# Top-k attention and a mixture of experts in one kernel: GpSimd's mask subtractions in halves, its row scaling in five parts

## The chip, the cores and the metric

The kernel runs on one core of one Trainium2 chip. The metric is the device time of one execution in microseconds; lower is better. Before the change it is 1338.02 us, the median of three runs (1337.96 to 1338.56).

A core has five engines that run their own instruction streams: TensorE (PE: matmuls and transposes), VectorE (DVE), ScalarE (ACT), GpSimd (POOL) and SyncE (SP, here the issuer of most DMAs). They meet through semaphores.

## The reference

```python
def _attn_ref(q, k, v):                       # batch 8, heads 8, seq 576, head_dim 64
    scores = scale * np.matmul(q, k.transpose(0, 1, 3, 2))
    kth = np.partition(scores, -32, axis=-1)[..., -32:-31]
    scores = np.where(scores >= kth, scores, -1e9)
    scores = scores - np.max(scores, axis=-1, keepdims=True)
    attn = np.exp(scores)
    attn = attn / (np.sum(attn, axis=-1, keepdims=True) + 1e-09)
    return np.matmul(attn, v)

def _moe_ref(x, w_gate, w1, w2):              # 4608 tokens of 512, 8 experts, hidden 1024
    logits = x @ w_gate
    expert_idx = np.argmax(logits, axis=1)
    probs = softmax(logits)
    gate_w = probs[np.arange(N), expert_idx]
    # each token goes to its one expert:
    y = np.maximum(x @ w1[e], 0.0) @ w2[e]
    return gate_w[:, None] * y
```

Each of 576 query rows of a head keeps its 32 largest scores of 576; softmax and the product with v follow. The heads of a token, side by side, are the 512 inputs of the expert layer. All is float32.

## The kernel before

**Attention.** Two heads of a batch form a unit (`P` = 128 rows of q and k hold both). Eight batches of four units make 32 units. A score tile has 128 queries on the partitions and 576 keys (`S`) along them; two tiles (`m` = 0, 1) go through the engines together as one step. A batch has 18 steps, the kernel 144. The score tile `s` is stored as `[128, m, 2, 288]`, the masked one `w` as `[128, m, 576]`; `HF` is 288.

What one step does, engine by engine:

- PE computes the scores (`products`, L292) and ACT copies them to `s` (L299), three steps ahead of their use (`AHEAD`).
- DVE finds the 32nd largest value of each row. It folds the row first: larger and smaller of the two halves (`fold`, L306 and L308, two operations with two 576-wide inputs), and again on the larger ones (`fold_on`, L314 and L316, with 288 columns). Then `search` takes the top eight four times (MAX8, L345 and L354), and takes them out between (MATCH_REPLACE8, L362). The folds of the next step stand in the last round of this one: L314, L316, two MAX8, then L306 and L308.
- ACT makes `low` from the threshold (L371), and from it `w`, which is zero where a score is kept and huge where it is not (`depths`, L387, one for each `m`).
- POOL subtracts: `w = s - w` (`less`, L396, one for each `m`). This is the mask subtraction. Then POOL makes a small check (`doubts`, L377, 6 columns) and, in the next step, `nbias` (L358, 2 columns).
- ACT takes the exponential with its row sum (`weights`, L404).
- PE transposes `w` one step later (`transposed`, L415, L427, L429); ACT copies the result (L422, L420, L437, L435).

**End of a unit.** `ending` runs beside the following steps at named places: PE multiplies by v (L450), ACT copies (L452), PE turns the result and multiplies it by the gate weights in the same product (L461), ACT copies both to `xl` (L468), and ACT and DVE make the reciprocals of the row sums `rz` (L472 to L479). At the place "rows", right after `less`, `doubts` and any stores of the step, POOL scales the logits (`logits`, L487, L489 or L492, L490) and then the unit's rows (`rows`, L500): five blocks `t` of 128 columns, each of two heads of 64, times a reciprocal that is the same for all 64 columns. `KC` is 5.

**Routing and experts.** After the fourth unit of a batch DVE picks the experts and places of its tokens (`choice`, `ranks`, `places`, `table`: L510 to L651, small operations put between the MAX8 and MATCH_REPLACE8 of a step one at a time), and POOL scatters the rows to memory by indirect DMA (L567). Blocks of 128 rows of one expert are fetched, and their matmuls (`block`, L893 and L910) are put into the steps of later batches in pieces, by a credit that is counted per step and not by time. What is left of them after the last step, and eight blocks of up to 192 rows (`long_block`, L829 and L850), is done at the end. POOL stores the results by indirect DMA (L808).

**What sets the order.** PE, ACT and DVE run in the order in which the program writes them (`manual_schedule`), and the POOL instructions of the steps are held to program order as well (`in_turn`). Buffers: `s` has 4, `w` 3, `few` and `low` 3.

Of the kernel before, what the change touches and what calls it, by code (L numbers as in the profile page):

```python
# [12 lines left out]
ALU = mybir.AluOpType  # L13
# [11 lines left out]
def _ins(ap: bass.AP, axis: int, n: int) -> bass.AP:  # L25
    dims = [list(d) for d in ap.ap]
    dims.insert(axis, [0, n])
    return bass.AP(tensor=ap.tensor, offset=ap.offset, ap=dims)
# [9 lines left out]
def _inner(ap: bass.AP, n: int) -> bass.AP:  # L38
    return _ins(ap, len(ap.ap), n)
# [3 lines left out]
def kernel(  # L43
# [47 lines left out]
    nc = tc.nc  # L91
# [5 lines left out]
    D = P // 2  # L97
# [3 lines left out]
    KC = NC + 1  # L101
    HF = S // 2
# [27 lines left out]
    k = SimpleNamespace()  # L130
# [74 lines left out]
    for n in range(2):  # L205
        t = const.tile([P, S if n else KC * P], F32, name=f"oT{n}")
# [3 lines left out]
        t = const.tile([P, NT + 1], F32, name=f"rz{n}")  # L210
# [36 lines left out]
    def in_turn(put):  # L247

        if not k.exact:
            tc.keep_in_program_order(put)  # L250
        return put
# [24 lines left out]
    def products(tiles):  # L276
        todo = []
        got = []
        for m, (n, i) in enumerate(tiles):
            ps = k.ps_s.tile([P, 2, SM], F32, name="sc")  # L280
            first = 0 if m and not tails(tiles) else ST
            if m and tails(tiles):
                todo += [(n, ps, h, slice((1 - h) * ST, (2 - h) * ST), cols, first) for h, _, cols in parts(i)]
            else:
                todo += [(n, ps, h, rows, cols, first) for h, rows, cols in parts(i)]
            got.append(ps)
        for half in range(2):
            for n, ps, h, rows, cols, first in todo:
                j = half ^ h if tails(tiles) else half
                d = slice(h * D, (h + 1) * D)  # L290
                keys = slice(first + j * HF, first + (j + 1) * HF)
                nc.tensor.matmul(ps[rows, j, 0:HF], n.q[d, cols], n.k[d, keys], start=True, stop=True)  # L292
        return got

    def scores(got):

        s = k.att.tile([P, 2, 2, HF], F32, name="s", bufs=2 if k.exact else 4)
        return s, [
            lambda m=m, ps=ps: nc.scalar.copy(s[:, m, :, :], ps[:, :, 0:HF]) for m, ps in enumerate(got)  # L299
        ]  # L300
# [82 lines left out]
    def depths(s, low):  # L383

        w = k.att.tile([P, 2, S], F32, name="w", bufs=1 if k.exact else 3)
        for m in range(2):
            nc.scalar.activation(  # L387
                w[:, m, :], s[:, m, :, :].rearrange("p j k -> p (j k)"), AF.Relu,
                scale=-STEEP, bias=low[:, m:m + 1],
            )  # L390
        return w

    def less(s, w):

        for m in range(2):
            k.last_pool = in_turn(nc.gpsimd.tensor_tensor(  # L396
                w[:, m, :], s[:, m, :, :].rearrange("p j k -> p (j k)"), w[:, m, :], op=ALU.subtract
            )).ins

    def weights(tiles, w, nbias):  # L400

# [92 lines left out]
    def rows(n, x):  # L494

        rzb = rz_of[n.u % 2][:, :].rearrange("p (t h) -> p t h", h=2)
        at = 0 if n.u % 2 else lw
        xu = x[:, :, n.u * P:(n.u + 1) * P].rearrange("p t (h d) -> p t h d", h=2)
        xl = n.xl[:, :, at:at + P].rearrange("p t (h d) -> p t h d", h=2)
        in_turn(nc.gpsimd.tensor_tensor(xu, xl, _inner(rzb, D), op=ALU.mult))  # L500

    def choice(lg):

# [433 lines left out]
    with fast:  # L937
# [185 lines left out]
        def loop():  # L1123
# [9 lines left out]
            for i, (b, g) in enumerate(work):  # L1133
# [12 lines left out]
                at_place("small")  # L1146
                w_of[i] = depths(s_of[i], low)
                less(s_of.pop(i), w_of[i])
                doubts()
                put_stores()  # L1150
# [71 lines left out]
    with ExitStack() as outer:  # L1222
# [10 lines left out]
        with ExitStack() as st:  # L1233
# [7 lines left out]
            with tc.For_i(0, B, 1) as b:  # L1241
# [3 lines left out]
                for u in range(0, U, 2):  # L1245
                    two = [load_unit(b, u), load_unit(b, u + 1)]
                    for n in two:
                        load_values(n)
                        open_unit(n)
                    for g in groups(u):  # L1250
                        tiles = [(two[a - u], tile) for a, tile in g]
                        s, steps = scores(products(tiles))
                        for step in steps:
                            step()
                        low, nbias, _ = search(tiles, s, None)
                        w = depths(s, low)
                        less(s, w)
                        weights(tiles, w, nbias)
                        for _ in transposed(tiles, w):
                            pass  # L1260
                        n, tile = tiles[0]
                        if tile == (NC - 1 if n.u % 2 else 2 * NC):
                            for _ in outputs(n, x):
                                pass
                            for _ in divisors(n):
                                pass
                            logits(n, lg)
                            rows(n, x)
# [69 lines left out]
```

## Time and profile before

| | |
|---|---|
| median of three runs | 1338.02 us |
| profiled execution, its own time | 1339.03 us |
| its span, first to last instruction | 1337.4 us |
| PE busy | 1189.3 us (89%) |
| DVE busy | 1076.6 us (81%) |
| ACT busy | 930.8 us (70%) |
| POOL busy | 661.9 us (49%) in 805 instructions |
| mask subtraction L396 | 288 times, 410.2 us |
| row scaling L500 | 32 times, 54.2 us |

"Busy" is the time in which an engine has an instruction under way; an instruction that is held up in mid-course counts as busy. Matmuls overlap in TensorE's pipeline and their ends are modelled. A group row gives line, engine, operation, result and inputs, shape and count; after the first bar stand the busy time in us and the mean of one in ns, after the second the engine's idle time before these instructions and what ended it. A timeline row gives start and duration in us.

### The profile page before, as it was taken

Reading aid. Unit: us, or ns where it says so; the run is one execution under the profiler, and the core shown is the slowest. Engines: PE = TensorE matmul, PEld = TensorE weight load, DVE = VectorE, ACT = ScalarE, POOL = GpSimd, SP = SyncE. Lnnn points to the kernel's source line nnn. Section 1 sums busy time; section 2 is a strip of 40 time slices with the busy share of each in tenths; the row PEclk is TensorE's granted clock in tenths of the full one; section 3 lists DMA queues with packets and bytes.
Section 4 is the critical chain, followed back from the end, with each engine's and each line's share of the span. In section 5 each row is a group of like instructions: output and inputs, shape, how many; then the busy total and the mean of one; then the engine's idle time right before and its main releaser. Section 6 shows DMA issues by size and latency. Waiting matters only on the chain. (4 is left out here: it accounts for less than half of the span.)

```text
span 1337.4 us, 24295 instructions
## 1 busy us (share of the span) xinstructions
PE 1189.3 (89%) x7570; PEld 831.4 (62%) x7570; DVE 1076.6 (81%) x4629; ACT 930.8 (70%) x2125; POOL 661.9 (49%) x805
## 2 busy tenths in 40 slices
PE   5667766766799999999999999999999999999995
PEld 3344443444466766676677666666677667699973
DVE  7999999999999999999999999999999932000000
ACT  4788788887888888888787888887778851111110
POOL 3454547555755665567555756475547642000000
PEclk9788788888899999999999999999999999999998
DMA  2000001001384348435855294329452739946790
GB/s 84 30 29 30 30 29 65 29 29 38 122 305 168 108 164 288 160 110 175 297 208 179 74 350 170 118 76 372 171 204 87 283 116 332 369 146 219 290 342 18
DMA packets 95563, 214.36 MB, mean 160 GB/s; under 512 B 4926, under 2 KB 25662, under 8 KB 95424
## 3 DMA queue, kind: packets, MB, share of 16 engines
q1 hardware_dynamic: 88800, 192.45, 40.8%
q0 software_dynamic: 6336, 19.97, 4.2%
q8 instruction: 61, 1.00, 0.3%
q14 instruction: 78, 0.64, 0.2%
q10 hardware_dynamic: 288, 0.30, 0.1%
HBM read 191.42 MB, written 21.80 MB: 159 GB/s over the span
## 5 line engine op out<-in xcount | busy, mean ns | idle before, releaser
L396 POOL TENSOR_TENSOR w<-s,w 128x576 f32<-128x576 f32 x288 | 410.2, 1444 | 418.4 <-ACT w L387 418.4
L893 PE MATMUL ph<-xTs,w 128*128 128x128 f32 x2048 | 250.2, 276 | 5.9 <-ACT xTs L790 5.9
L893 PEld LDWEIGHTS ph<-xTs,w 128*128 128x128 f32 x2048 | 239.1, 192 | 21.9 <-issue 14.6
L910 PE MATMUL py<-w,hT 128*128 128x512 f32 x512 | 236.2, 597 | 0.0
L404 ACT ACTIVATE w<-w,nbias 128x576 f32<-128x576 f32 x288 | 224.1, 792 | 3.0 <-POOL w L396 2.0
L292 PE MATMUL sc<-qkb 64*128 64x288 f32 (+1 forms) x1280 | 206.0, 473 | 9.5 <-ACT s L299 5.1
L387 ACT ACTIVATE w<-s,low 128x576 f32<-128x576 f32 x288 | 207.6, 768 | 4.7
L415 PE MATMUL wTm<-turn,w 128*128 128x128 f32 x1152 | 170.1, 287 | 32.0 <-ACT xl L468 21.4
L415 PEld LDWEIGHTS wTm<-turn,w 128*128 128x128 f32 x1152 | 132.0, 145 | 92.5 <-issue 34.4
L299 ACT COPY s<-sc 128x576 f32<-128x576 f32 x288 | 168.9, 640 | 10.4 <-PE sc L292 10.4
L1217 DVE CAST any_i<-pd 1x1 int32<-1x1 f32 x1 | 0.1, 145 | 207.9 <-PE pd L1215 207.9
L422 ACT COPY wT<-wTm 128x512 f32<-128x512 f32 x256 | 139.2, 604 | 39.3 <-PE wTm L415 39.2
L354 DVE MAX8 tops<-scr 128x8 f32<-128x168 f32 x576 | 162.8, 317 | 0.0
L450 PE MATMUL po<-wT,vb 128*64 128x288 f32 x1024 | 154.9, 450 | 0.4 <-ACT wTt L437 0.4
L354 DVE MAX8 tops<-few 128x8 f32<-128x144 f32 (+1 forms) x576 | 154.4, 300 | 0.0
L292 PEld LDWEIGHTS sc<-qkb 64*128 64x128 f32 (+1 forms) x1280 | 110.1, 195 | 65.4 <-issue 25.6
L910 PEld LDWEIGHTS py<-w,hT 128*128 128x128 f32 x512 | 90.7, 190 | 90.4 <-issue 89.2
L808 POOL DMA_INDIRECT out_dram<-y,xg x40 | 42.6, 1066 | 189.8 <-ACT y L869 82.5
L345 DVE MAX8 few<-l 128x8 f32<-128x288 f32 x288 | 127.3, 442 | 0.0
L450 PEld LDWEIGHTS po<-wT,vb 128*64 128x64 f32 x1024 | 74.2, 150 | 77.3 <-issue 26.0
L306 DVE TENSOR_TENSOR h<-s 128x576 f32<-128x576 f32 x144 | 114.8, 797 | 3.9 <-ACT s L299 3.7
L308 DVE TENSOR_TENSOR l<-s 128x576 f32<-128x576 f32 x144 | 108.0, 750 | 0.0
(175 smaller groups left out, 1649.8 us busy)
## 6 DMA issues: line engine op xcount, KB each, us to landing
w<-in_moe_w_dram SPq DMA_DIRECT2D x72, 2048.0 KB, 8.6
qkb<-in_qk_dram SPq DMA_DIRECT2D x31, 608.0 KB, 5.8
vb<-in_v_dram SPq DMA_DIRECT2D x32, 320.0 KB, 3.1
xg<-x_rows SPq DMA_DIRECT2D x36, 257.0 KB, 10.6
x_rows<-blank SPq DMA_DIRECT2D x5, 257.0 KB
x_rows<-blank POOLq DMA_DIRECT2D x4, 257.0 KB, 8.2
x_rows<-x,posi POOLq DMA_INDIRECT x40, 3.1
out_dram<-y,xg POOLq DMA_INDIRECT x40, 4.5
```

Source lines behind the costliest of these rows:

```text
L292: nc.tensor.matmul(ps[rows, j, 0:HF], n.q[d, cols], n.k[d, keys], start=True, stop=True)
L299: lambda m=m, ps=ps: nc.scalar.copy(s[:, m, :, :], ps[:, :, 0:HF]) for m, ps in enumerate(got)
L345: nc.vector.max(out=f.few[:, m, QF + 8 * j:QF + 8 * j + 8], in_=away)
L354: nc.vector.max(out=tops[:, m, r * 8:(r + 1) * 8], in_=src[m])
L387: nc.scalar.activation(w[:, m, :], s[:, m, :, :].rearrange("p j k -> p (j k)"), AF.Relu, scale=-STEEP, bias=low[:, m:m + 1],)
L396: k.last_pool = in_turn(nc.gpsimd.tensor_tensor(w[:, m, :], s[:, m, :, :].rearrange("p j k -> p (j k)"), w[:, m, :], op=ALU.subtract)).ins
L404: nc.scalar.activation(w[:, m, :], w[:, m, :], AF.Exp, scale=scale, bias=nbias[:, m:m + 1], accum_out=n.z[:, c:c + 1])
L415: nc.tensor.transpose(pm[:, c * P:(c + 1) * P], w[:, m, first:first + P], ident)
L422: nc.scalar.copy(wT[:, :, m, q], pm4)
L450: nc.tensor.matmul(po[r, 0:HF], n.v[:, c, r], rhs, start=(c == 0), stop=(c == KC - 1))
L893: nc.tensor.matmul(ph[:, f, :], n.w1[:, 0, dt, fc * P:(fc + 1) * P], n.xT[:, dt, :], start=(dt == 0), stop=(dt == DT - 1),)
L910: nc.tensor.matmul(py, hT[:, f, :], n.w2[:, 0, f, :], start=(f == 0), stop=(f == FT - 1))
```

## The change

`less` issues each mask subtraction as two of 288 columns, 576 instructions instead of 288. `rows` issues the scaling of a unit's rows as five instructions of 128 columns, 160 instead of 32. The same elements are computed from the same inputs by the same engine. One further line each moves later lines of the file by one or two. The scheduler of the framework, which places the waits from the tiles' regions, adds a wait on an earlier ACT instruction ahead of most exponentials (L404) and a wait on POOL ahead of 363 of the transposes (L415).

```diff
     def less(s, w):
 
         for m in range(2):
-            k.last_pool = in_turn(nc.gpsimd.tensor_tensor(
-                w[:, m, :], s[:, m, :, :].rearrange("p j k -> p (j k)"), w[:, m, :], op=ALU.subtract
-            )).ins
+            for j in range(2):
+                part = w[:, m, j * HF:(j + 1) * HF]
+                k.last_pool = in_turn(nc.gpsimd.tensor_tensor(part, s[:, m, j, :], part, op=ALU.subtract)).ins
...
     def rows(n, x):
...
         xl = n.xl[:, :, at:at + P].rearrange("p t (h d) -> p t h d", h=2)
-        in_turn(nc.gpsimd.tensor_tensor(xu, xl, _inner(rzb, D), op=ALU.mult))
+        for t in range(0, KC):
+            in_turn(nc.gpsimd.tensor_tensor(xu[:, t], xl[:, t], _inner(rzb[:, t], D), op=ALU.mult))
```

## The prediction

> **What bounds the kernel now.** I read the busy shares by time slice first, then a table of windows, then the groups of GpSimd (POOL) and VectorE (DVE), then the timeline where those two meet, then the waits.
>
> ```profile
> DVE  7999999999999999999999999999999932000000
> ACT  4788788887888888888787888887778851111110
> POOL 3454547555755665567555756475547642000000
> ```
>
> For 32 of 40 slices DVE has no free tenth; POOL is half idle. POOL's own time is therefore not the bound; what it does to DVE or to ScalarE (ACT) is. The windows (busy us by engine, then TensorE's granted clock) show where TensorE (PE) is full as well.
>
> ```profile
> 0.00:370.00 370.00, 256.99 (x1464) 153.87 (x1465) 362.66 (x1578) 289.95 (x671) 198.94 (x265) 0.86 0.15 48
> 370.00:650.00 280.00, 272.37 (x1862) 190.31 (x1862) 279.66 (x1223) 239.23 (x553) 165.44 (x202) 1.00 0.55 195
> 650.00:750.00 100.00, 99.35 (x650) 67.83 (x650) 96.64 (x393) 80.63 (x187) 62.83 (x70) 1.00 0.49 173
> 750.00:950.00 200.00, 195.18 (x1329) 136.08 (x1321) 197.93 (x829) 167.69 (x386) 124.04 (x144) 1.00 0.58 205
> 950.00:1065.00 115.00, 113.77 (x768) 79.02 (x765) 111.79 (x466) 92.26 (x214) 70.26 (x80) 1.00 0.50 177
> 1065.00:1337.40 272.40, 251.58 (x1516) 204.31 (x1514) 27.91 (x147) 60.99 (x119) 40.41 (x48) 0.97 0.65 232
> ```
>
> To 370 us DVE alone is full. From 370 to 650 it still is (0.3 us idle), with PE idle for 7.6 us. From 650 to 750 and from 950 to 1065 PE is nearly full: 0.65 and 1.2 us idle. After 1065 PE works alone. So a microsecond saved on DVE before 650 ends the kernel a microsecond earlier; later no more can be had than PE's idle time.
>
> The groups have busy us and mean ns after the bar.
>
> ```profile
> L396 POOL TENSOR_TENSOR w<-s,w 128x576 f32<-128x576 f32 x288 | 410.2, 1444 | 418.4 <-ACT w L387 418.4
> L500 POOL TENSOR_TENSOR x<-xl,rz 128x640 f32<-128x640 f32 x32 | 54.2, 1695 | 0.0
> ...
> L377 POOL TENSOR_TENSOR doubt<-few,tops 128x6 f32<-128x6 f32 x144 | 35.5, 247 | 0.0
> ```
> ```profile
> L306 DVE TENSOR_TENSOR h<-s 128x576 f32<-128x576 f32 x144 | 114.8, 797 | 3.9 <-ACT s L299 3.7
> L308 DVE TENSOR_TENSOR l<-s 128x576 f32<-128x576 f32 x144 | 108.0, 750 | 0.0
> ...
> L314 DVE TENSOR_TENSOR few<-h 128x288 f32<-128x288 f32 x144 | 78.4, 544 | 0.0
> L316 DVE TENSOR_TENSOR hl<-h 128x288 f32<-128x288 f32 x144 | 71.6, 497 | 0.0
> ```
>
> The medians of these four DVE lines are 0.735, 0.746, 0.444 and 0.447 us. Times 144 that leaves 9.0 + 0.6 + 14.5 + 7.2 = 31 us above the median. Five small operations of the routing tables (L613, L637, L512, L633, L552) hold another 12 us. So about 43 us of DVE's "busy" time is standing still. The timeline shows why (POOL first, then DVE).
>
> ```profile
> 665.65 3.00 POOL L396 TENSOR_TENSOR w<-s,w 128x576 f32<-128x576 f32 x2 [2.06 <-ACT w L387]
> ```
> ```profile
> 666.02 1.35 DVE L314 TENSOR_TENSOR few<-h 128x288 f32<-128x288 f32 x1
> 667.30 1.66 DVE L316 TENSOR_TENSOR hl<-h 128x288 f32<-128x288 f32 x1
> 668.89 0.56 DVE L354 MAX8 tops<-scr 128x8 f32<-128x168 f32 x2
> 669.37 0.73 DVE L306 TENSOR_TENSOR h<-s 128x576 f32<-128x576 f32 x1
> ```
>
> L314 arrives 0.37 us into the first mask subtraction and ends 0.32 us after it; L316 then waits for the whole second one and ends 0.31 us after that. A DVE operation with two inputs stands until POOL's instruction is over, and the next POOL instruction goes before the next DVE operation: they take turns. MAX8 beside a subtraction keeps its 0.28 to 0.32 us. Such meetings are spread over the windows as 5.3, 7.6, 10.0, 10.6 and 9.1 us of standing.
>
> **The price of a piece.** A 576-column subtraction takes 1.41 us when nothing disturbs it, a 6-column one (L377) 0.20. That is 2.12 ns a column and about 0.185 us fixed. A half is then 0.80 us, with some 0.6 us in which DVE is shut out; pieces follow each other 0.04 us before the last one's end, so a step's two subtractions grow from 2.78 to 3.08 us. L500 undisturbed takes 1.255 us; by the same fixed part a fifth takes 0.40 us, 0.2 of it closed to DVE, and the five 1.84. POOL's added time is 144 x 0.30 + 32 x 0.58 = 62 us, beside the 418 us that it idles before L396. Bounds: no fixed part at all gives 0.70 a half and no growth; 0.25 us gives 0.83 and 0.25 us a half more closed time than none. I take 0.185, since three shapes lie on that line (L487, 80 columns with the same broadcast, takes 0.32).
>
> The Trainium skill ("GPSIMD Engine Reference", Instruction dispatch) counts one indirect call of tens of cycles for each instruction; at 50 cycles of its 1.2 GHz that would be, as an estimate, 0.04 us. By it the halves would grow the step by under 0.1 us, no operation would be hit anew, and the sum below would be nearer 8 us than 5. The 0.20 us for 6 columns speaks for the dearer price.
>
> **The halves.** Per meeting, with turns taken piece by piece:
> - L314 and L316 both hit (665.65 and three like it): before 0.91 + 1.21 = 2.12 us. Now L314 waits 0.30, L316 0.60, and the pair left over reaches L306 (0.06) and L308 (0.60): 1.56. Saves 0.56, four times 2.2. Six more where L316, L306 or L633 waits behind a first hit save 0.3 to 0.6: 2.7.
> - L314 alone hit by the second subtraction (nine): that ends 0.30 later and L316 is now hit too; each loses 0.1 to 0.3: -1.6. Six steps in which L314 came less than 0.30 us after POOL was done are hit now: -0.8.
> - The small table operations, now behind a half: nine at 0.3 to 0.6: 4.2.
> - In an undisturbed step nothing meets: POOL ends 1.8 us before L314, then 1.5.
>
> Net 6.7 us of DVE.
>
> **The rows in five.** Eight units have L314 0.52 to 0.58 us into L500 (0.56 us stall). The row work now begins 0.30 later: L314 0.02, L316 0.20, L306 0.06, L308 0.20, together 0.48; saves 0.6 in all. Seven have L306 at +1.35 (0.6 us); now 0.28: saves 2.2. Two at 72 and 203 us save 1.2. But five units, where L500 was pushed behind L306 and L308 (2.49 us long), now start the next subtraction 0.57 us later and end it 0.87 later, where L314 had 0.38 us of room: -2.4. Net 1.6.
>
> **What of it counts.** By window the 8.3 us are 0.9, 1.1, 2.9, 1.1 and 2.4. All of the first two counts. In 650 to 750 PE's idle 0.65 is the limit, then 1.1, then 1.2. Sum 4.8 us.
>
> **Costed at nothing.** The build gives each exponential (L404) one more wait, on ACT's own earlier write, as 280 semaphore instructions (17 ns each in this trace, 4.8 us on an engine 16% idle), and 363 transposes (L415) a wait for POOL. Where a transpose's wait is already met the trace shows 109 ns to the next start, with or without it. These waits are met a step earlier. L404 itself has room: in the early steps it starts 1.03 us after the first subtraction and 0.44 after the second. The added 0.15 and 0.30 fit; behind it ACT still has the wait shown here, about 1 us a time.
>
> ```profile
> ACT low L371 <- DVE tops L354: 63.0, 60, 4.1
> ```
>
> If both covers were gone, the 52 steps before 370 us would pay up to 0.30 each, 16 us.
>
> **Sum.** The profiled execution took 1339.03 us (span 1337.4, 1.6 around it); the median of the runs, 1338.02, lies 1.0 below. 1339.03 - 4.8 = 1334.2 in the profile, 1333.2 as a median.
>
> **Rivals.**
> 1. *Nothing that can be told* (0.2%, 2.7 us, is about what a measurement of this kernel can tell). For it: the closed time of POOL is not made less, only cut, and two operations are hit where one was; PE is full for 215 of the later 415 us. If the singles and the five pushed units cost as worked out and the small operations meet again at the next half, 6.7 + 1.6 - 4.2 = 4.1 is left, of which some 2 count: 1336.
> 2. *Slower: the fixed part is closed to DVE too.* If a fifth shuts DVE out for 0.4 us rather than 0.2 and a half for 0.8, taking turns makes the four DVE operations pay four pieces: a row meeting costs 0.1 + 3 x 0.4 = 1.3 instead of 0.56. Twenty meetings lose 0.7 each, 14 us, 5 of them before 370; the mask halves gain nothing. It decides once a fifth closes more than about 0.25 us. Against it: L314 starts again 0.12 us before POOL's record ends, and POOL's next record loses only 0.22 us to a DVE operation of 0.44. Some 6 us would count: 1344.
> 3. *Much faster: all of it counts.* If turns are not taken and DVE passes between any two pieces (as L314 and L316 both went ahead of L500 at 331 us), a stall is at most the rest of one piece; stalls fall by more than half, 25 us. PE's idle caps the later part at 14, with 3 early: 1321.
>
> **Chances.** Forecast (over 2.7 us faster) 0.48, rival 3 0.08, rival 1 0.25, rival 2 0.19. The range runs from 1325 (rival 3 half true, 13 us) to 1341 (rival 2 half true): most of the first three cases and the mild half of the second.
>
> **What would show it.** Right: halves of about 0.80 us and fifths of 0.40; L314 below 510 ns mean, L316 near its 497, L308 above 750; POOL busy near 720 us; L404's wait for POOL still a few us; DVE's end near 1061. Wrong: halves over 0.85, L308 or L316 rising by more than L314 falls, L404 waiting for POOL by tens of us, or DVE freed while PE ends at the same time.

## The result and the profile after

The changed kernel takes 1341.18 us (median of nine runs, 1339.62 to 1342.4) against 1337.96 for the kernel before beside it (nine runs, 1337.42 to 1339.19): ratio 1.0022, 95% interval 1.0012 to 1.0033. It is 3 us slower. The forecast was 1333.2, and the range ended at 1341. A second set of nine runs (`after_same` below) gave 1341.41 and 1.0024 (1.0014 to 1.0033). The profiled execution took 1340.56 us, its span 1338.9.

From the page of the changed kernel, the busy shares by slice:

```profile
DVE  7999999999999999999999999999999942000000
ACT  4887878877888888888787888887788851111210
POOL 3565758665866686668666867596658651000000
```

VectorE (DVE) is as full as before, in the same slices; GpSimd (POOL) has more to do. The table of windows (columns as before: length, busy us of PE, PEld, DVE, ACT and POOL, TensorE's granted clock) gives the same stretches:

```profile
0.00:370.00 370.00, 261.44 (x1464) 155.83 (x1465) 363.05 (x1580) 291.30 (x672) 228.12 (x405) 0.85 0.15 49
370.00:650.00 280.00, 273.24 (x1864) 190.63 (x1864) 279.95 (x1218) 240.01 (x554) 189.78 (x308) 1.00 0.54 195
650.00:750.00 100.00, 99.35 (x650) 67.66 (x649) 96.29 (x395) 80.52 (x186) 69.79 (x108) 1.00 0.49 174
```

Up to 370 us DVE has done 1580 instructions where it had done 1578: in the stretch where every microsecond counts, next to nothing was won. The groups (busy us, mean ns of one, idle before) and two rows of the waits (us in total, times, longest) say what POOL's pieces cost and whom they meet:

```profile
L398 POOL TENSOR_TENSOR w<-s,w 128x288 f32<-128x288 f32 x576 | 455.4, 821 | 336.6 <-ACT w L387 168.6
L501 POOL TENSOR_TENSOR x<-xl,rz 128x128 f32<-128x128 f32 x160 | 84.3, 558 | 0.0
...
L306 DVE TENSOR_TENSOR h<-s 128x576 f32<-128x576 f32 x144 | 108.1, 751 | 2.4 <-ACT s L299 1.9
L308 DVE TENSOR_TENSOR l<-s 128x576 f32<-128x576 f32 x144 | 115.3, 800 | 0.0
L314 DVE TENSOR_TENSOR few<-h 128x288 f32<-128x288 f32 x144 | 75.0, 521 | 0.0
L316 DVE TENSOR_TENSOR hl<-h 128x288 f32<-128x288 f32 x144 | 73.4, 510 | 0.0
```
```profile
ACT low L371 <- DVE tops L354: 50.6, 55, 4.1
...
ACT w L404 <- POOL w L398: 12.2, 20, 1.1
```

L306 and L314 lost 6.7 and 3.4 us, L308 and L316 gained 7.3 and 1.8. The four together stand at 371.8 us; before they stood at 372.8. The standing was handed to the next operation, not removed. POOL's busy time grew by 84.5 us to 746.4. ScalarE's exponentials (L404) now wait for POOL for 12.2 us, where the trace before has 2.0 (5 times); its wait for the threshold (L371) fell from 63.0 to 50.6 us.

The meeting that the prediction showed, at 666 us, first POOL, then DVE:

```profile
665.45 4.05 POOL L398 TENSOR_TENSOR w<-s,w 128x288 f32<-128x288 f32 x4 [1.72 <-ACT w L387]
```
```profile
666.16 0.45 DVE L314 TENSOR_TENSOR few<-h 128x288 f32<-128x288 f32 x1
666.53 1.05 DVE L316 TENSOR_TENSOR hl<-h 128x288 f32<-128x288 f32 x1
667.50 0.56 DVE L354 MAX8 tops<-scr 128x8 f32<-128x168 f32 x2
667.98 0.87 DVE L306 TENSOR_TENSOR h<-s 128x576 f32<-128x576 f32 x1
668.77 1.35 DVE L308 TENSOR_TENSOR l<-s 128x576 f32<-128x576 f32 x1
```

Each piece of POOL and each two-input operation of DVE go in turn, as predicted: L314 passes, L316 waits 0.60 for a half, L306 0.13, L308 0.60. Here 1.34 us are lost where 2.12 were. The same at 100 us, where the folds meet the five parts of the rows:

```profile
99.99 2.80 POOL L501 TENSOR_TENSOR x<-xl,rz 128x128 f32<-128x128 f32 x5
```
```profile
100.28 0.44 DVE L314 TENSOR_TENSOR few<-h 128x288 f32<-128x288 f32 x1
100.64 0.65 DVE L316 TENSOR_TENSOR hl<-h 128x288 f32<-128x288 f32 x1
101.69 0.83 DVE L306 TENSOR_TENSOR h<-s 128x576 f32<-128x576 f32 x1
102.45 0.95 DVE L308 TENSOR_TENSOR l<-s 128x576 f32<-128x576 f32 x1
```

One more thing shows only behind the last matmul. From there to the end of the span it is 18.23 us, and was 15.30. Between two instructions of POOL's closing sequence there is a pause of 3.17 us, and the second of them then takes 43 ns, so that it waited for no semaphore itself:

```
last instructions of POOL: start (us) and what, profiled executions
                      before     changed kernel   changed, second set
branch                1323.09    1321.68          1322.31
3 semaphores, last    1326.58    1325.77          1326.30
next semaphore        1326.65    1328.95          1329.76
```

The last matmul itself ended at 1320.67 us, 1.4 us earlier than in the profile of before.

### The profile page after: what moved, and what is told of

Its sections match the earlier page's. It is cut to its first block, busy times and chain, and to the rows that moved or that the text cites. A ratio compares the mean times of both kernels' runs of the same rounds, so it can differ in the third digit from the quotient of the medians.

```text
span 1338.9 us, 25177 instructions
## 1 busy us (share of the span) xinstructions
PE 1193.6 (89%) x7570; PEld 832.9 (62%) x7570; DVE 1076.7 (80%) x4629; ACT 933.4 (70%) x2125; POOL 746.4 (56%) x1221
## 5 line engine op out<-in xcount | busy, mean ns | idle before, releaser
L398 POOL TENSOR_TENSOR w<-s,w 128x288 f32<-128x288 f32 x576 | 455.4, 821 | 336.6 <-ACT w L387 168.6
L404 ACT ACTIVATE w<-w,nbias 128x576 f32<-128x576 f32 x288 | 224.2, 791 | 13.3 <-POOL w L398 12.2
L415 PE MATMUL wTm<-turn,w 128*128 128x128 f32 x1152 | 173.7, 288 | 33.5 <-ACT xl L468 21.0
L415 PEld LDWEIGHTS wTm<-turn,w 128*128 128x128 f32 x1152 | 133.5, 147 | 95.6 <-issue 59.4
L299 ACT COPY s<-sc 128x576 f32<-128x576 f32 x288 | 169.1, 641 | 10.6 <-PE sc L292 10.6
L308 DVE TENSOR_TENSOR l<-s 128x576 f32<-128x576 f32 x144 | 115.3, 800 | 0.0
L306 DVE TENSOR_TENSOR h<-s 128x576 f32<-128x576 f32 x144 | 108.1, 751 | 2.4 <-ACT s L299 1.9
```

Of the source, the lines that this page charges most:

```text
L398: k.last_pool = in_turn(nc.gpsimd.tensor_tensor(part, s[:, m, j, :], part, op=ALU.subtract)).ins
L404: nc.scalar.activation(w[:, m, :], w[:, m, :], AF.Exp, scale=scale, bias=nbias[:, m:m + 1], accum_out=n.z[:, c:c + 1])
L415: nc.tensor.transpose(pm[:, c * P:(c + 1) * P], w[:, m, first:first + P], ident)
```

## The experiments

Every ratio is to the kernel before, run beside it on the same chip (1337.9 to 1338.6 us). All variants but `after_same` and `rows_three_plain` have some one-column memsets on GpSimd in the branch that is never taken, ahead of the end of the program; they are not executed and only shift where the end lies.

**The two parts alone.** `halves_alone` has L500 as before; `rows_alone` has whole mask subtractions.

```diff
 halves_alone
-        for t in range(0, KC):
-            in_turn(nc.gpsimd.tensor_tensor(xu[:, t], xl[:, t], _inner(rzb[:, t], D), op=ALU.mult))
+        in_turn(nc.gpsimd.tensor_tensor(xu, xl, _inner(rzb, D), op=ALU.mult))
 rows_alone
-            for j in range(2):
-                part = w[:, m, j * HF:(j + 1) * HF]
-                k.last_pool = in_turn(nc.gpsimd.tensor_tensor(part, s[:, m, j, :], part, op=ALU.subtract)).ins
+            k.last_pool = in_turn(nc.gpsimd.tensor_tensor(
+                w[:, m, :], s[:, m, :, :].rearrange("p j k -> p (j k)"), w[:, m, :], op=ALU.subtract
+            )).ins
```

Expected of `halves_alone`:

> Only the mask subtractions are in halves; the row scaling is whole; GpSimd's end lies where it did before, modulo 128 (66 memsets in the branch that is never taken). By the prediction's sum the halves give VectorE 6.7 us, of which some 3 us should count: 1335. If the small routing operations meet one half after another, as the profile of the changed kernel shows, 2.5 us are left and 1 us counts: 1337. Theory B, that the pieces cost more than they free: 1339 to 1341.

Expected of `rows_alone`:

> Only the row scaling is in five parts; the mask subtractions are whole; GpSimd's end lies where it did before, modulo 128 (106 memsets in the branch that is never taken). By the prediction the rows give VectorE 1.6 us, and without the halves' longer steps ahead of them the five pushed units should lose less: 1336 to 1338. Theory B, that four operations pay for four parts at 0.4 us each: 1340 or more.

Measured: halves alone 1342.83 us, 1.0029 (1.0017 to 1.0042); rows alone 1335.26 us, 0.9975 (0.9966 to 0.9984). The two parts pull against each other: the halves cost 4 us (by the interval 2.3 to 5.6), the rows in five win 3.3. Both lie outside what was expected first: the halves are slower than 1339 to 1341, the rows faster than 1336 to 1338. The runs of the halves spread from 1340 to 1347, and their profile is the run of 1346.68. It shows one way in which they lose. Its timeline at a meeting with the whole row scaling:

```profile
100.87 1.26 POOL L500 TENSOR_TENSOR x<-xl,rz 128x640 f32<-128x640 f32 x1
```
```profile
101.14 1.31 DVE L314 TENSOR_TENSOR few<-h 128x288 f32<-128x288 f32 x1
```

In the trace before, L314 came 0.57 us into L500 here and took 1.00 us:

```profile
100.40 1.26 POOL L500 TENSOR_TENSOR x<-xl,rz 128x640 f32<-128x640 f32 x1
```
```profile
100.97 1.00 DVE L314 TENSOR_TENSOR few<-h 128x288 f32<-128x288 f32 x1
```

Now the pair of subtractions ends later, L500 starts later, L314 comes only 0.27 us into it and stands 0.3 us longer.

**The end of the program.** `after_shifted` is the changed kernel with 46 of the memsets, `after_shifted_128` with 128, `before_shifted` the kernel before with 80, `after_same` the changed kernel unaltered, once more.

```diff
+            pad = keep.tile([P, 1], F32, name="pad")
+            for _ in range(46):
+                nc.gpsimd.memset(pad, 0.0)
```

Expected of `after_shifted`:

> The changed kernel, with 46 one-column memsets on GpSimd put into the branch that is never taken, so that GpSimd's last instructions lie at the same place modulo 128 instructions as in the kernel before. No executed instruction is changed. Theory A (the loss is a wait for instructions at GpSimd's very end): the 3.2 us pause between two of its last semaphore instructions goes, and the time falls by about 3 us, to 1338 or a little below (1336.5 to 1338.5). Theory B (the loss lies in the attention steps, where pieces shut VectorE out): the time stays at 1341.

Expected of `before_shifted`:

> The kernel before, with 80 one-column memsets on GpSimd in the branch that is never taken, so that GpSimd's last instructions lie where they lie in the changed kernel, modulo 128. Nothing of the change is in it. Theory A: a pause of about 3 us appears after GpSimd's third instruction behind the final branch, and the time rises by about 3 us, to 1340.5 to 1341.5. Theory B: the time stays at 1338.0.

Expected of `after_shifted_128`:

> The changed kernel with 128 never-executed memsets ahead of the program's end on GpSimd, where 46 took the pause of 3.2 us away. If the place of the end within blocks of 128 instructions sets the pause, it is back: a tail of 18.2 us from the last matmul and about 1341.2. If the pause belongs to one layout only, a tail of 15.3 us and about 1339.4.

Expected of `after_same`:

> The changed kernel once more, unaltered, for its end: if the pause of 3.2 us behind GpSimd's last store belongs to this layout, the profile shows it again (18.2 us from the last matmul to the end of the span) and the time is again 2 to 3 us above the two shifted versions (1339.4 and 1338.6); if it was one execution, 15.3 us and about 1339.

| | us | ratio (95%) | last matmul to end of span |
|---|---|---|---|
| after_shifted | 1339.39 | 1.0005 (0.9996 to 1.0014) | 15.25 |
| after_shifted_128 | 1338.60 | 1.0005 (0.9996 to 1.0014) | 15.20 |
| after_same | 1341.41 | 1.0024 (1.0014 to 1.0033) | 18.40 |
| before_shifted | 1338.91 | 1.0002 (0.9993 to 1.0011) | 15.56 |

The unaltered kernel has the pause in both of its profiles (3.17 and 3.44 us), neither shifted version has it, and both are faster: 1.0023 less 1.0005 of 1338 is 2.4 us. So most of the measured loss of 3 us comes from where the program's end happens to lie, and without it the change is worth nothing that can be told (0.7 us, interval -0.5 to 1.9). At 1339.39 us `after_shifted` lies above the 1336.5 to 1338.5 expected of it: the pause accounts for less than the whole loss. The expectation that the kernel before could be given the pause by a shift failed, and so did the one that a shift by 128 instructions brings it back. What sets the place stays open: in the two profiles with the pause, packets of the two instruction queues move during its first half (1325.8 to 1327.2 and 1326.9 to 1328.1 us), but kernels without a pause (`rows_three_plain`, both shifted versions) have such packets at their ends too.

**Why the halves cost: a longer step, or the cut.** `spaced_between` leaves the subtractions whole, keeps the rows in five, and puts two subtractions of one column between the two of a step; `spaced_after` puts them behind the pair. No wait is added on any other engine.

```diff
+    bit = doubt[:, B * U - 1, NT - 1, 0:1]
...
             )).ins
+            if m == 0:
+                for _ in range(2):
+                    in_turn(nc.gpsimd.tensor_tensor(bit, bit, bit, op=ALU.subtract))
```

> The rows in five and whole mask subtractions, with two added GpSimd subtractions of one column between the two of each step (on a spare column that the last step overwrites). They make the second subtraction and all that follows it on GpSimd end about 0.27 us later, as the halves do, with nothing cut and no wait added on any engine. Theory 'longer step': the halves cost 4 us in both earlier pairs (1342.8 against 1338.9, 1339.4 against 1335.3) because the step's GpSimd work ends 0.27 us later; then this kernel loses the same, about 1339.3 (ratio 1.0005). Rival 'the cut itself': the cost comes from two operations of VectorE hit where one was and from the 280 and 197 added semaphore instructions of ScalarE and TensorE; then this kernel stays near 1335.3 (ratio 0.9975).

Expected of `spaced_after`:

> The same two one-column subtractions behind the pair instead of between: the masked scores are ready as early as in the rows in five alone, and only the checks, the rows and what follows on GpSimd come 0.27 us later. If the cost of a longer step lies in later rows that hold VectorE, about 1338 to 1339; if it lies in ScalarE's exponentials, which wait for the second subtraction, about 1335.5; by the rival 'the cut itself' also 1335.5.

Their times, 4606.59 and 4603.90 us, say nothing: the spare column was read by the kernel's check for doubtful rows as a doubt, and its exact pass ran behind the first. The first pass is whole in the traces. Its end is where VectorE's cast of the check starts; the rows are those of `rows_alone`, `spaced_after` and `spaced_between`:

```profile
1318.34 0.15 DVE L1218 CAST any_i<-pd 1x1 int32<-1x1 f32 x1 [208.34 <-PE pd L1216]
```
```profile
1319.91 0.14 DVE L1222 CAST any_i<-pd 1x1 int32<-1x1 f32 x1 [208.18 <-PE pd L1220]
```
```profile
1323.71 0.15 DVE L1223 CAST any_i<-pd 1x1 int32<-1x1 f32 x1 [208.21 <-PE pd L1221]
```

Two tiny operations behind the pair cost 1.6 us, between the two subtractions 5.4 us. In the four profiles of the changed kernel's instructions (two unaltered, two shifted) the same place lies between 1320.35 and 1323.12 us, so 1.6 us is not clear of chance and 5.4 is. Behind the pair, the tiny operations delay the checks and the rows but not the second subtraction, and the exponentials wait 7.9 us for POOL (7.0 in `rows_alone`, 13.4 in `spaced_between`). What costs is thus mainly that the second subtraction ends later, not that rows and checks move behind it.

`spaced_between_2` takes the spare column from a place that the last step overwrites, so that its time can be read.

```diff
-    bit = doubt[:, B * U - 1, NT - 1, 0:1]
+    bit = doubt[:, B * U - 1, 2 * NC - 1, 0:1]
```

> spaced_between again, with the spare column taken from a place that the last step overwrites, so that nothing behind the first pass runs. In the earlier profile the first pass ended 5.4 us later than that of rows_alone, with VectorE's stalls at 52.6 us instead of 41.0. Theory 'longer step': 1339 to 1341 (ratio 1.001 to 1.002), as the halves. Rival 'the cut itself and its added waits': 1335.3 (ratio 0.9975).

Measured: 1341.09 us, 1.0024 (1.0015 to 1.0033). Against rows alone that is 0.0049, 6.6 us, more than the halves cost. The reason lies in the size of the spacer, which I had put at 0.27 us. From its timeline:

```profile
96.15 1.46 POOL L398 TENSOR_TENSOR w<-s,w 128x576 f32<-128x576 f32 x1 [3.03 <-ACT w L387]
97.58 0.46 POOL L403 TENSOR_TENSOR doubt<-doubt 128x1 f32<-128x1 f32 x2
97.99 1.40 POOL L398 TENSOR_TENSOR w<-s,w 128x576 f32<-128x576 f32 x1
```

From the start of a step's first subtraction to the end of its last the medians over 144 steps are 2.79 us in `rows_alone`, 3.08 with the halves and 3.21 here: 0.28 and 0.42 us longer. The halves cost 4.0 us on top of the rows in five (1.0005 for the shifted changed kernel, 0.9975 for rows alone; each interval is 0.0009 either side) and 3.9 without them (1.0029). 4.0 for 0.28 and 6.6 for 0.42 are 14 and 16 us of the kernel's time for each microsecond by which a step's subtractions are longer; 4.0 and 6.6 are each known to about 1.7 us. A step made longer with nothing cut costs about as much for each microsecond, so the halves' loss needs neither the cut nor the semaphore instructions that come with it (in the trace of the changed kernel 258 more on ScalarE and 205 more on TensorE than before; the recorded texts have 280 and 197). The spacer also adds two pieces that DVE can meet, so part of its cost may be theirs; the likeness of the two rates is no proof of their equality.

VectorE's standing, taken from each trace as time above the median of the four folds and above the shortest of each small operation, sums it up (us, and number of operations hit):

| hit by | before | rows_alone | after | spaced_between_2 | rows_three |
|---|---|---|---|---|---|
| mask: L314 | 8.9 (15) | 10.6 (23) | 10.8 (32) | 16.0 (31) | 9.3 (16) |
| mask: L316 | 7.3 (6) | 7.3 (6) | 7.2 (12) | 0 | 7.3 (6) |
| mask: L306 and L308 | 4.1 (4) | 4.5 (5) | 6.1 (18) | 8.4 (9) | 4.2 (5) |
| mask: small operations | 11.4 (16) | 12.7 (16) | 12.9 (34) | 18.9 (21) | 14.5 (21) |
| mask, all | 31.7 (41) | 35.1 (50) | 37.0 (96) | 43.3 (61) | 35.3 (48) |
| rows, all | 11.2 (18) | 3.7 (27) | 4.7 (28) | 6.0 (40) | 1.8 (9) |

From `rows_alone` to the changed kernel the hits by a mask subtraction go from 50 to 96 and their sum from 35.1 to 37.0: half as long, twice as many, and a little over. With the rows' 1.0 that is 2.9 us more standing, of the 4.0 that the halves cost.

A second account of the same traces asks whether VectorE was held up in other ways. From the start to the end of the last fold (the last L308) it is busy for 1047.2 us and idle for 17.5 in `rows_alone`, 1051.1 and 16.4 in the changed kernel, 1057.9 and 12.1 in `spaced_between_2`. It comes later because it is longer busy, not because it waits more; nothing here shows that the longer waits of the exponentials or the added semaphore instructions held it up. In the profile of `halves_alone`, its slowest run, they may have: there the idle time too is longer than before, 19.8 us against 16.3.

**The rows in other numbers of parts.** All with whole mask subtractions: three parts of 256, 256 and 128 columns, with and without the memsets, and two of 384 and 256.

```diff
-        for t in range(0, KC):
+        for t in (slice(0, 2), slice(2, 4), slice(4, 5)):      # rows_three, rows_three_plain
+        for t in (slice(0, 3), slice(3, 5)):                   # rows_two
```

> Whole mask subtractions, the rows in three parts of 256, 256 and 128 columns. By taking turns piece by piece a row meeting costs VectorE at most about 0.4 us where the fifths cost 0.2 and the whole 0.56, so the row stalls of 11.1 us before (3.8 with five) come to about 6; the row work is 0.3 to 0.4 us shorter than in five. I expect between: 1335.5 to 1337. If the shorter row work is what counts, under 1335; if only small pieces help, 1338.

Expected of `rows_two`:

> Whole mask subtractions, the rows in two parts of 384 and 256 columns: two added instructions a unit less than in five, one less than in three. If short row work is what counts, 1333 to 1334, as three or better; if the length of a piece counts (a meeting costs up to 0.6 us again), 1335 to 1337.

Expected of `rows_three_plain`:

> rows_three without the memsets that are never executed: 1333.8 as with them, or up to 3 us more if this layout has the pause at its end.

Measured: three parts 1333.76 us, 0.9968 (0.9956 to 0.9980); without the memsets 1335.25, 0.9971 (0.9961 to 0.9982); two parts 1337.79, 0.9997 (0.9987 to 1.0006); five were 0.9975. Three parts are the fastest kernel here, better than before and after by 4 and 7 us, though not told from five by these intervals. They beat what was expected between (1335.5 to 1337); two parts miss both of their cases (1333 to 1334 and 1335 to 1337). Neither the number of pieces nor their length alone orders the rows' standing (11.2 us whole, 10.0 in two parts, 1.8 in three, 3.7 in five); where a boundary falls would, as far as this meeting shows. `rows_three` at the meeting of 100 us:

```profile
99.45 3.45 POOL L501 TENSOR_TENSOR x<-xl,rz 128x256 f32<-128x256 f32 x3
```
```profile
100.00 0.47 DVE L314 TENSOR_TENSOR few<-h 128x288 f32<-128x288 f32 x1
100.37 0.47 DVE L316 TENSOR_TENSOR hl<-h 128x288 f32<-128x288 f32 x1
```

L314 comes 0.55 us into the rows, about where the first part of 256 columns ends; it passes, L316 follows, and POOL is the one that stands. The rows' hits fall to 1.8 us. With two parts the first is still running then, and the rows' standing stays at 10.0 us (11.1 before by the same count).

## Why the prediction was wrong, point by point

- **Price of a piece: right.** Predicted 0.80 us a half, 0.40 a fifth, 3.08 a pair; measured medians 0.80, 0.40 and 3.08. L501's mean of 558 ns holds the pieces that DVE made wait; with these POOL's busy time came to 746.4 us, not to near 720: the 62 us of added work were of undisturbed pieces. From start to start a subtraction takes 1.378 us whole and 0.757 in halves, so 0.136 us of it do not shrink with the columns. The Trainium skill ("GPSIMD Engine Reference", Instruction dispatch) counts tens of cycles for the dispatch; at 0.04 us, the prediction's estimate from it, the pair would have grown by 0.08 us. It grew by 0.28, and the measurement decides for the dearer price.
- **Turns piece by piece: right.** The 666 us meeting lost 1.34 us where 1.56 was worked out; L314, which was to wait 0.30, came just as the first half ended. At a row meeting (100 us) L316, L306 and L308 stand 0.20, 0.10 and 0.20, and L314 nothing: 0.50 where 0.48 was predicted. Rival 2, the fixed part closed to DVE too, is refuted by the same rows; rival 3 falls with the turns.
- **The rows: mechanism right, gain too small.** Net 1.6 us of DVE was predicted, 4.0 gross and 2.4 lost to later subtractions. Alone they took the rows' hits from 11.2 to 3.7 us and raised those of the masks by 3.4: 4.1 net, and 3.3 in time. The gross gain of 4.0 was little more than half of the 7.5 that came, the loss 1 us too small.
- **The halves: the step that failed.** Net +6.7 us was predicted, and the sum of mask hits rose by 1.9 us over that of the rows alone. Three terms fail. The small table operations were to save 4.2 us; they save nothing (12.7 and 12.9 us), because they come in a row and the one after the delayed one meets the next half: 16 hits became 34. The doubles were to save 4.9; L316 kept its sum in twice the hits (7.3 and 7.2 us), and what left L306 (6.7 us by the group rows) came back on L308 (7.3). The cost of a longer step was worked out for fifteen steps (2.4 us), from meetings that the trace before showed. With next to nothing saved, the halves' loss of about 4 us is put down to this cost, which the spacers show to be large enough: 14 to 16 us of the kernel's time for each microsecond by which every step's subtractions end later. L314 meets a mask 32 times where it did 15 times before, 23 with the rows alone.
- **Costed at nothing.** L404's wait for POOL went from 2.0 us to 12.2 in the changed kernel (7.0 with the rows alone), so the room of 0.44 us did not always cover 0.30. VectorE's idle time did not grow with it (17.5 us with the rows alone, 16.4 in the changed kernel), so no part of it is seen to reach VectorE there. The added semaphore instructions need no share in the loss, as the spacers show, but they were not taken away by themselves.
- **What of it counts.** All early DVE time was to count. At the end of the 49th step, near 360 us, DVE was 0.6 us ahead of the trace before instead of the 0.9 for that stretch; by 446 us nothing of it is left, and TensorE's matmuls then stay within 0.4 us of those before until 1056 us. The 4.8 us that were to count came to none. (The prediction's own terms, 0.9, 1.1, 0.65, 1.1 and 1.2, add up to 4.95, not 4.8; the forecast hardly moves by it.)
- **Not in the sum at all:** the pause at the end, 2.4 us by the runs. Without it the outcome is rival 1, nothing that can be told, and by the mechanism that it names: closed time that is cut and not made less, and small operations that meet the next half. Rival 1's own figure, 1336, still lies below the 1338.6 and 1339.4 of the shifted versions.

By the runs: -3.3 for the rows, +4.0 for the halves, +2.4 for the pause make +3.1; measured +3. This divides the loss and does not test the division, since the 4.0 and the 2.4 are themselves differences from the changed kernel. What tests it is `halves_alone`, which gives 3.9 for the halves from other runs.

## What to carry to other kernels

Where two engines take turns on something, ask before cutting the long instruction of one into pieces how many operations the other has in a row: here each of them met a piece, and the fixed part of the added pieces made every step's work end later. By these runs cutting paid in the rows (three parts 4 us, five parts 3.3), where in the trace before L314 comes 0.52 to 0.58 us after their start eight times, and not in the mask subtractions, into which it comes after anything from 0.10 to 1.37 us. That the boundary has to lie at the moment of arrival is what one meeting and the two-part run suggest; three and five parts were not told apart in time. And before a difference of 0.2% is put down to the work, compare the time from the last matmul to the end.

## What the hardware showed that was not expected

- The end of a program can cost 3.2 us more or less with its layout: POOL's pause of 3.17 and 3.44 us between two semaphore instructions, in both profiles of the unaltered changed kernel and in no other.
- A GpSimd subtraction of a single column that writes what it reads holds the next one back by 0.21 us (mean 209 ns, 288 of them), as much as one of 6 columns lasts (0.20 us).
- The runs of `rows_three_plain` fall in two groups: three at 1332.9 us with a mean granted clock of 0.955 or 0.956, five at 1335.1 to 1336.1 with 0.944 to 0.952. In its profile, one of the latter, the clock granted from 1040 to 1100 us is 0.97, in that of `rows_three` 1.00, and from the 6000th to the 6400th matmul record it takes 67.2 us against 65.5. The profile of before has 0.97 in this window and those of the changed kernel and of rows alone 1.00, so 1.4 us of earlier last matmul in the changed kernel is not a gain of the change: against `before_shifted`, which ended its last matmul at 1320.82, it is 0.15.
